# Values of three leading blocks by SyncE's queue, and the first 230 tasks in a new order

## The chip, the core and the metric
The kernel runs on one core of a Trainium2 chip. Its engines are PE (TensorE: matrix products and transposes into PSUM), ACT (ScalarE), DVE (VectorE), POOL (GpSimd) and SP (SyncE, which here only issues DMAs). A DMA issued by POOL is written by software and can cast fp32 to bf16 on its way; one issued by SP or ACT goes through the hardware's queue and leaves the type as it is. All of them use the same 16 DMA engines. The metric is device microseconds of one launch; lower is better.

## The reference
Attention with a sliding window of 128 positions and a linear bias by distance, for 8 batches, 8 heads, 576 positions, head size 64; its output goes through a two-layer network with a squared ReLU.

```python
scores = scale * np.matmul(q, k.transpose(0, 1, 3, 2))
rel = pos[:, None] - pos[None, :]
bias = slopes[:, None, None] * (-np.abs(rel).astype(np.float32))[None, :, :]
mask = (rel >= 0) & (rel < window)
scores = np.where(mask, scores + bias[None], -1000000000.0)
...
attn = np.exp(scores)
attn = attn / (np.sum(attn, axis=-1, keepdims=True) + 1e-09)
attn_out = np.matmul(attn, v).astype(np.float32)
...
x = np.ascontiguousarray(attn_out.transpose(0, 2, 1, 3)).reshape(B * S, H * D)
h = x @ w_in                       # [4608, 512] x [512, 2048]
g = np.maximum(h, 0.0) ** 2
out = (g @ w_out).astype(np.float32)   # [4608, 2048] x [2048, 512]
```

## The kernel before
All of it is one program. The tokens are cut into blocks of up to 128 positions of one batch with all 8 heads. For a block, K, Q and V are loaded as bf16 tiles; K and Q are turned (on PE for the first eight blocks, by DMA for later ones), scores and values follow, and the normalised x [128, 512] is turned for the network. There groups of 512 tokens are multiplied by w_in, pass ReLU and square, and are multiplied by w_out.

Every piece of work is a task, `plan.add({engine: cost}, key, emit, deps, slots to take, slots to give back)`. Nothing is scheduled at run time: the string `ORDER` (lines 62 to 200) names all 1709 tasks in one order, with the engine of each (`a` ACT, `d` DVE, `g` POOL, `s` SP, nothing for PE) and the PSUM banks or buffers that it takes. Each engine's instructions stand in that order, and an engine waits at an instruction until what it needs is there, with everything behind it.

The names of the tasks that matter here, for a block m:
- `lk`, `lq`, `lv`: the loads of K, Q and V. For block 0, `lk0.r` and `lq0.r` go by SP's and ACT's queues in fp32, in halves and in pieces of 1 KB, into a staging tile (a part of `wsum`, which has no other use until much later), and `ck0`, `cq0` cast them. All other loads go by POOL's queue with the cast in the DMA. A tile is 128 positions of 8 heads of 64: 1024 pieces of 256 B in fp32. V lands in `vf`, which also has a column of ones per head.
- `tp m.i` (L690): K (i = 0) or Q (i = 1) turned on PE into a bank; `ev m.i` (L428 on DVE, L430 on ACT): the copy to `kqf`.
- `b m` (L805): the biases of a block into two banks, and `s m` (L814): its scores on top of them. This is the function `lone`, for blocks 0 to 3, which are the first of a batch's positions and look only at themselves.
- `e m.r` (L823): the exponentials to P; `pv m.h` (L874): P times V; `r`, `n` (L888, L901): the reciprocal of the sum and the product that gives x; `xp` (L921): x turned; `x m`: its copy to `xT`.
- `w_in n`: w_in in five pieces, two of 256 columns and three of 512; `u g.r.e` (L1021): for 128 tokens r of group g the up products with piece e of that row; for row 0, `u0.0.0` and `u0.0.1` need w_in 0 and w_in 1, for the other rows `u0.r.0` needs both of these and `u0.r.1` needs w_in 2.

PE's order before begins: warm-up, b0, tp0.0, tp2.0, b2, tp0.1, tp2.1, tp3.0, tp1.0, s2, s0, b1, tp1.1, pv2.0, pv0.0, pv0.1, s1, tp3.1, xp0, pv2.1, pv1.0, pv1.1, b3, u0.0.1, xp2, s3, u0.0.0, xp1, u0.2.0.

POOL's DMAs take turns on eight semaphores, so that POOL waits at a load for the one eight before it. PSUM has eight banks; a task that takes a bank waits for whoever reads it last.

Of the kernel before, what the change touches and what calls it, by code (L numbers as in the profile page):

```python
# [63 lines left out]
slope1.1:d slope0.1:a slope1.3:a ck0:a slope0.2:a warm::0 b0::1,2 lk2:g lq2:g lq0.0:s lq0.1:s lk1:g cq0:a one0.0:d  # L64
tp0.0::0 tp2.0::3 b2::4,5 tp0.1::6 tp2.1::7 ev2.0.0:d ev0.1.0:a lk3:g lq1:g tp3.0::3 ev3.0.0:a ev2.1.0:d ev0.0.0:d
one0.2:d tp1.0::6 s2 s0 e0.0:a e2.0:a e2.1:a ev1.0.0:d e0.1:a lv0:g lv2:g lq3:g lv1:g w_in1:g w_in0:g w_in2:g lv3:g
w_in3:g lk4:g lq4:g b1::0,3 tp1.1::6 pv2.0::4 ev1.1.0:d r2.0:d pv0.0::6 pv0.1::2 s1 n2.0:d r0.1:d r0.0:d n0.0:d
tp3.1::4 n0.1:d xp0.0::2 pv2.1::6 x0.0:d r2.1:d ev3.1.0:d mask1.1:a e1.0:a e1.1:a table:a pv1.0::0 pv1.1::3 b3::5,1
n2.1:d u0.0.1::2 r1.0:d r1.1:d n1.0:d n1.1:d xp2.0::6 s3 u0.0.0::0 xp1.0::3 dist0:d x2.0:a e3.0:a x1.0:a mask1.7:a
reluu0.0.0:a:0 u0.2.0::6 mask0.3:a mask1.2:a mask0.1:a mask1.6:a e3.1:a u0.1.0::3 u0.1.1::0 pv3.0::1 pv3.1::5  # L70
u0.2.1::4 u0.0.2::7 squ0.0.0:d one1.2:d reluu0.1.0:a:0 mask0.2:a reluu0.2.0:a:1 one1.8:d r3.0:d squ0.1.0:d one1.7:d
r3.1:d n3.0:d n3.1:d xp3.0::5 x3.0:d one1.5:d reluu0.2.1:a:0 one1.6:d squ0.2.1:d squ0.2.0:d reluu0.1.1:a:2 mask1.5:a
mask1.4:a mask0.7:a mask0.5:a mask1.3:a mask1.0:a reluu0.0.2:a:3 u0.1.2::0 tp4.0::5 tp4.1::7 ev4.1.0:d squ0.0.2:d
u0.2.2::4 ev4.0.0:a reluu0.0.1:a:1 s4.0::7,2 s4.1::5,1 reluu0.1.2:a:0 e4.0:a lk5:g reluu0.2.2:a:3 lk6:g lq5:g lv5:g
lq6:g w_in4:g tp5.0::0 u0.0.3::6 u0.3.0::4 tp5.1::7 squ0.0.1:d one1.1:d one1.0:d squ0.1.2:d ev5.0.0:d e4.1:a mask0.0:a
mask0.4:a mask0.6:a m4.0:d ev5.1.0:d squ0.1.1:d lk7:g lv4:g lv6:g lq7:g w_out3:g w_out0:g lv7:g w_out2:g w_out1:g
e4.3:a reluu0.3.0:a:0 e4.2:a reluu0.0.3:a:1 squ0.3.0:d u0.3.1::2 tp6.0::7 reluu0.3.1:a:0 ev6.0.0:d tp6.1::4 s5.0::5,1
# [238 lines left out]
def kernel(  # L316
    ctx: ExitStack, tc: tile.TileContext, q, k, v, moe_w_in, moe_w_out, out
):
    nc = tc.nc
# [243 lines left out]
    def load_block(m, key, v_key=None):  # L563
# [56 lines left out]
        def fetch_v():  # L620
            nc.gpsimd.dma_start(tile_of(s_v[m])[0:n, :, 0:D], source(v, m))  # L621
# [859 lines left out]
```

## Time and profile before

| | |
|---|---|
| median of 3 runs | 287.59 us (287.37 to 289.48) |
| the profiled execution | 288.0 us, its span from the first to the last instruction 285.9 us |
| granted TensorE clock | 0.997 |
| PE busy | 277.0 us, 97% of the span |
| DVE busy | 247.1 us, 86% |
| ACT busy | 207.5 us, 73% |
| POOL busy | 106.3 us, 37% |

The difference of 2.1 us between the profiled execution's time and its span lies before the first and behind the last instruction. The shares are means over the whole program; the change lies in the first 25 us, in which PE starts its warm-up at 2.5 us and useful work at 7.5 us. The times of the profile are microseconds from the start of the span. A row of the timeline gives a start, a duration, the engine, the line, the operation and the tiles, and in brackets the idle time before it and who ended it; consecutive instructions of one kind share a row.

### The profile page before, as it was taken

To read this page: it belongs to the slowest core of one execution; us is meant where nothing else is said; L and a number is where in the kernel's file an instruction comes from. 1 tells how busy PE (TensorE), PEld (TensorE's weight loads), DVE (VectorE), ACT (ScalarE), POOL (GpSimd) and SP (SyncE) were. 2 spreads that over 40 slices of the span, in tenths; PEclk is the share of its full clock that TensorE was granted. 3 is DMA by queue.
4 is the path that set the end of the run, shared out by engine and by line. 5 is a ranking of instruction groups with operands and counts; after the bars stand their busy time and mean duration, and the time that the engine had idled before them with its cause. 6 is when DMAs were issued, how large, how long until landed. Compare 5 with 4: busy or idle time off the path is not lost.

```text
span 285.9 us, 8500 instructions
## 1 busy us (share of the span) xinstructions
PE 277.0 (97%) x3403; PEld 240.0 (84%) x3404; DVE 247.1 (86%) x566; ACT 207.5 (73%) x408; POOL 106.3 (37%) x132
## 2 busy tenths in 40 slices
...
GB/s 126 161 197 167 183 201 165 171 172 148 206 145 250 131 172 129 149 207 130 203 135 150 139 174 164 170 164 157 148 93 39 40 73 3 0 111 39 53 79 127
DMA packets 169062, 39.08 MB, mean 137 GB/s; under 512 B 154560, under 2 KB 169024, under 8 KB 169024
## 3 DMA queue, kind: packets, MB, share of 16 engines
...
q8 instruction: 26, 0.43, 0.7%
q10 hardware_dynamic: 592, 0.46, 0.6%
q14 instruction: 12, 0.10, 0.1%
...
## 4 chain that ended last, share of the span: by engine, by line
PE 95%; ACT 2%; DVE 1%; issue 0%; POOL 0%; DVEq 0%; POOLq 0%
PE o L1271 38%; PE h L1116 30%; PE h L1021 9%; PE s L745 6%; PE pv L874 5%; PE wm L662 2%; PE xp L921 1%; PE tp L690 1%; ACT P L823 1%; ACT rt L988 1%; PE pv L856 1%; PE o L1373 0%; PE s L805 0%; ACT masks L475 0%; PE pv L851 0%; PE s L814 0%
## 5 line engine op out<-in xcount | busy, mean ns | idle before, releaser
L1271 PEld LDWEIGHTS <-g 128*128 128x128 bf16 x704 | 67.3, 98 | 9.0
L777 ACT ACTIVATE P<-s 128x512 bf16<-128x512 f32 x120 | 64.7, 613 | 5.7 <-PE s L745 3.3
L430 ACT ACTIVATE f<-h 128x512 f32<-128x512 f32 x74 | 42.5, 601 | 25.8 <-PE h L1116 25.5
L1137 DVE CUSTOM_DVE_ANT_0 rt<-h,f 128x512 bf16<-128x512 f32 x84 | 56.4, 684 | 4.9 <-ACT f L430 1.7
L980 ACT ACTIVATE g<-rt 128x512 bf16<-128x512 bf16 x79 | 48.4, 634 | 6.4 <-DVE rt L1137 5.9
L1271 PE MATMUL o<-w_out_sb,g 128*128 128x256 bf16 x432 | 52.3, 273 | 0.0
L1116 PE MATMUL h<-xT,w_in_sb 128*128 128x256 bf16 x336 | 46.9, 273 | 0.0
L1116 PEld LDWEIGHTS <-w_in_sb 128*128 128x128 bf16 x448 | 42.2, 98 | 5.6
...
L988 ACT ACTIVATE rt<-h 128x512 bf16<-128x512 f32 (+1 forms) x61 | 35.2, 599 | 8.6 <-PE h L1116 3.9
L1271 PE MATMUL o<-wsum,sums 128*128 128x256 bf16 x288 | 35.5, 273 | 0.0
L1116 PEld LDWEIGHTS <-us 128*128 128x128 bf16 x336 | 31.9, 98 | 4.3 <-DVE ut L1085 0.2
L1271 PE MATMUL o<-wsum,g 128*128 128x256 bf16 x272 | 34.5, 273 | 0.0
L772 DVE TENSOR_TENSOR P<-P,masks 128x1024 bf16<-128x1024 bf16 x48 | 32.2, 680 | 1.3 <-ACT masks L475 0.8
L1116 PE MATMUL h<-ut,us 128*128 128x256 bf16 x224 | 31.1, 273 | 0.0
L1021 PE MATMUL h<-xT,w_in_sb 128*128 128x128 bf16 (+1 forms) x384 | 30.8, 237 | 0.1
L982 DVE TENSOR_TENSOR g<-rt 128x512 bf16<-128x512 bf16 (+1 forms) x66 | 26.1, 413 | 4.7 <-ACT rt L988 4.4
L1271 PEld LDWEIGHTS <-sums 128*128 128x128 bf16 x288 | 27.5, 98 | 3.1
L901 DVE TENSOR_TENSOR x<-pv,rec 128x256 bf16<-128x256 f32 x72 | 28.7, 417 | 0.7
L1021 PEld LDWEIGHTS <-w_in_sb 128*128 128x128 bf16 x384 | 27.0, 98 | 2.3 <-issue 0.2
L621 POOL DMA_DIRECT2D vt<-in_v_dram x28 | 25.0, 908 | 7.8 <-PE pv L856 5.3
L430 ACT ACTIVATE f<-o 128x512 f32<-128x512 f32 x29 | 17.3, 599 | 11.0 <-PE o L1271 10.0
...
## 6 DMA issues: line engine op xcount, KB each, us to landing
out_dram<-f SPq DMA_DIRECT2D x62, 128.0 KB, 3.9
kq<-in_k_dram POOLq DMA_DIRECT2D x31, 128.0 KB, 6.4
kq<-in_q_dram POOLq DMA_DIRECT2D x31, 128.0 KB, 7.2
vt<-in_v_dram POOLq DMA_DIRECT2D x28, 128.0 KB, 7.5
w_out_sb<-in_moe_w_out_dram POOLq DMA_DIRECT2D x4, 512.0 KB, 11.6
w_in_sb<-in_moe_w_in_dram POOLq DMA_DIRECT2D x3, 512.0 KB, 8.6
...
vf<-in_v_dram POOLq DMA_DIRECT2D x4, 128.0 KB, 4.9
```

The costliest lines, as they stand in the source:

```text
L430: nc.scalar.activation(o, i, AF.Copy)
L621: nc.gpsimd.dma_start(tile_of(s_v[m])[0:n, :, 0:D], source(v, m))
L772: nc.vector.tensor_tensor(flat(Pt[sP.idx], w), flat(Pt[sP.idx], w), flat(mk, w), op=ALU.mult)
L777: nc.scalar.activation(flat(Pt[sP.idx], slice(2 * i, 2 * i + 2)), sS[i].tile.rearrange("p (j t) -> p j t", j=2)[:, :, lo:hi], AF.Exp, bias ...
L901: nc.vector.tensor_tensor(o, heads(sv)[0:n, :, 0:D], sr.tile[0:n, :].unsqueeze(2).to_broadcast([n, 4, D]), op=ALU.mult)
L980: nc.scalar.activation(o, i, AF.Square, bias=0.0, scale=1.0)
L982: nc.vector.tensor_tensor(o, i, i, op=ALU.mult)
L988: nc.scalar.activation(rts[srt.idx][:, 0:n], slot.tile[:, 0:n], AF.Relu, bias=0.0, scale=1.0)
L1021: nc.tensor.matmul(slot.tile[:, f * w:(f + 1) * w], w_in_sb[:, cc, fc * 128:(fc + 1) * 128], xT[:, cc, lo % (XR * 128):lo % (XR * 128) + w ...
L1116: nc.tensor.matmul(slot.tile[:, j * 256:j * 256 + 256], a, b_, start=fresh and j == 0 and c == 0, stop=c == 1, skip_group_check=True)
L1137: nc.vector._custom_dve(TENSOR_ADD_SAT, out=rts[srt.idx], in0=slot.tile, in1=other(), s0=FMAX, s1=0.0)
L1271: nc.tensor.matmul(slot.tile[:, z * 256:z * 256 + 256], stationary(c), moving(c), start=fresh and z == 0 and c == 0, stop=c == F - 1, skip ...
```

## The change
A constant `V_HW = (0, 2, 1)` names three blocks. For these, `load_block` no longer issues V by POOL; SP issues it in fp32 into one of the three staging tiles that were free, and a new task `cv` casts it to `vf`. Blocks 0, 2 and 1 get stages 1, 2 and 3. K and Q of block 0 stay as they are, but `cq0` is on DVE now and not on ACT.

```diff
+V_HW = (0, 2, 1)
...
         def fetch_v():
             nc.gpsimd.dma_start(tile_of(s_v[m])[0:n, :, 0:D], source(v, m))
+        if m in V_HW:
+            st, s_sv = stages[1 + V_HW.index(m)][:, 0:d_model], Slot(f"stage{1 + V_HW.index(m)}")
+            l_v = plan.add({"SP": 720.0}, key + 0.2 if v_key is None else v_key,
+                           lambda: nc.sync.dma_start(st[0:n].rearrange("s (h d) -> s h d", h=H), source(v, m)), [],
+                           [s_sv], dma=700.0, lat=1500.0, name=f"lv{m}")
+            c_v = plan.add({"DVE": 590.0, "ACT": 480.0}, key + 0.2 if v_key is None else v_key,
+                           lambda: copy(c_v, tile_of(s_v[m])[0:n, :, 0:D], st[0:n].rearrange("s (h d) -> s h d", h=H)),
+                           [l_v], [s_v[m]], [s_sv], name=f"cv{m}")
+            t_load[m] = c_v
+            t_v[m] = [c_v, t_one["v0", m]]
+            return
         l_v = plan.add({"POOL": 890.0}, key + 0.2 if v_key is None else v_key, fetch_v, [], [s_v[m]],
```

The string `ORDER` is written anew for about the first 230 tasks; behind them the order is the same, with other bank and buffer numbers. Two lines of it, from the first loads to the scores of block 2:

```diff
+cq0:d tp0.0::0 tp0.1::3 cv2:d cv0:a tp2.0::4 tp2.1::5 ev2.1.0:d one0.2:d lk3:g ev0.1.0:a ev0.0.0:a lv1:s lq3:g w_in1:g
+w_in0:g w_in2:g lv3:g w_in3:g lk4:g lq4:g ev2.0.0:d b2::6,7 s0 e0.0:a e0.1:a b3::4,0 s2 one0.0:d pv0.0::1 tp1.0::5
```

PE's order now begins: warm-up, b0, tp0.0, tp0.1, tp2.0, tp2.1, b2, s0, b3, s2, pv0.0, tp1.0, tp1.1, tp3.0, b1, pv2.1, pv2.0, pv0.1, s1, xp2, pv1.0, xp0, tp3.1, pv1.1, u0.2.0, u0.0.1, s3, u0.0.0, xp1, u0.2.1. Bias 3 takes banks 4 and 0, of which 4 held tp2.0. Later on, a touch of ACT's table moves from block 1's exponentials to block 7's, and three of the four w_out loads go behind the load of K and Q of block 8.

On DVE, at its first copies, there stood (kqf<-tp is a copy of turned K or Q, the MEMSETs write ones in vf):

```order
9 L513 TENSOR_SCALAR sums<-sums 128x128
10 L522 MEMSET vf 128x8
11 L428 COPY kqf<-tp 128x512 x3
12 L522 MEMSET vf 128x8
13 L428 COPY kqf<-tp 128x512 x2
14 L888 RECIPROCAL rec<-pv 128x4
15 L901 TENSOR_TENSOR x_114<-pv,rec 128x4x64
```

and now:

```order
9 L514 TENSOR_SCALAR sums<-sums 128x128
10 L429 CAST kq_71<-wsum 128x2x4x64
11 L429 CAST vf<-wsum 128x8x64
12 L429 COPY kqf<-tp 128x512
13 L523 MEMSET vf 128x8
14 L429 COPY kqf<-tp 128x512
15 L523 MEMSET vf 128x8
16 L429 COPY kqf<-tp 128x512 x2
17 L900 RECIPROCAL rec<-pv 128x4
18 L913 TENSOR_TENSOR x_114<-pv,rec 128x4x64
```

Rows 10 and 11 are `cq0` and `cv2`; the copies in rows 12 and 14, both of block 2, stand behind them. On ACT, where the copies of block 0 are now, there stood from its first cast on:

```order
4 L430 ACTIVATE kq_71<-wsum 128x2x4x64
5 L515 ACTIVATE sums<-sums 128x128
6 L430 ACTIVATE kq_71<-wsum 128x2x4x64
7 L430 ACTIVATE kqf<-tp 128x512 x2
8 L823 ACTIVATE P_111<-s_154 128x512
9 L823 ACTIVATE P_112<-s_175 128x512
10 L823 ACTIVATE P_112<-s_177 128x512
11 L823 ACTIVATE P_111<-s_156 128x512
```

and now:

```order
4 L431 ACTIVATE kq_71<-wsum 128x2x4x64
5 L516 ACTIVATE sums<-sums 128x128
6 L431 ACTIVATE vf<-wsum 128x8x64
7 L431 ACTIVATE kqf<-tp 128x512 x2
8 L835 ACTIVATE P_111<-s_154 128x512
9 L835 ACTIVATE P_111<-s_156 128x512
10 L835 ACTIVATE P_112<-s_204 128x512
11 L835 ACTIVATE P_112<-s_206 128x512
12 L431 ACTIVATE vf<-wsum 128x8x64
```

Row 6 is `cv0` in the place of `cq0`, and the two copies of row 7 are both of block 0 (before, of blocks 3 and 0). Rows 8 and 9 are block 0's exponentials, now together and ahead of block 2's; row 12 is `cv1`. On POOL the loads ahead of w_in were

```order
8 L610 DMA kq_72<-in_k_dram 128x8x64
9 L610 DMA kq_72<-in_q_dram 128x8x64
10 L610 DMA kq_73<-in_k_dram 128x8x64
11 L610 DMA kq_74<-in_k_dram 128x8x64
12 L610 DMA kq_73<-in_q_dram 128x8x64
13 L621 DMA vf<-in_v_dram 128x8x64 x2
14 L610 DMA kq_74<-in_q_dram 128x8x64
15 L621 DMA vf<-in_v_dram 128x8x64
16 L543 DMA w_in_sb<-in_moe_w_in_dram 128x4x256 x2
```

and are

```order
8 L611 DMA kq_72<-in_k_dram 128x8x64
9 L611 DMA kq_72<-in_q_dram 128x8x64
10 L611 DMA kq_73<-in_k_dram 128x8x64
11 L611 DMA kq_73<-in_q_dram 128x8x64
12 L611 DMA kq_74<-in_k_dram 128x8x64
13 L611 DMA kq_74<-in_q_dram 128x8x64
14 L544 DMA w_in_sb<-in_moe_w_in_dram 128x4x256 x2
```

The three V loads left for SP, where they stand in the order 0, 2, 1 right behind block 0's Q (kq_72, 73 and 74 are blocks 2, 1 and 3).

More of the change, by code (lines that the diff above doesn't have):

```diff
@@ L63 @@
 iota:g ident:d dist1:d slope1.0:d warm0:d lk0.1:a lk0.0:s one0.1:d slope0.3:d slope1.2:a slope0.0:a one0.3:d
[L64 to L77, printed above, removed]
@@ L198 @@
-st8.7.3:s st7.3.0:s st7.3.1:s p8.3.0 p8.3.1 p8.4.0::3 p8.4.1::7 p8.4.1b::0 c12_8:d st8.3.1:s c21.1.0_8:d c21.0.0_8:d
-st8.4.1:s st8.4.0:s st8.3.0:a c21.1.128_8:d st8.4.1b:a
+slope1.1:d slope0.1:a slope1.3:a ck0:a slope0.2:a warm::0 b0::1,2 lk2:g lq2:g lq0.0:s lq0.1:s lv0:s lv2:s lk1:g lq1:g
+cq0:d tp0.0::0 tp0.1::3 cv2:d cv0:a tp2.0::4 tp2.1::5 ev2.1.0:d one0.2:d lk3:g ev0.1.0:a ev0.0.0:a lv1:s lq3:g w_in1:g
+w_in0:g w_in2:g lv3:g w_in3:g lk4:g lq4:g ev2.0.0:d b2::6,7 s0 e0.0:a e0.1:a b3::4,0 s2 one0.0:d pv0.0::1 tp1.0::5
@@ new lines @@
+e2.0:a e2.1:a ev1.0.0:d tp1.1::3 ev1.1.0:d tp3.0::2 cv1:a r0.0:d n0.0:d b1::5,6 pv2.1::7 pv2.0::3 pv0.1::1 s1 r2.1:d
+r2.0:d n2.0:d n2.1:d e1.0:a e1.1:a r0.1:d ev3.0.0:d n0.1:d xp2.0::7 pv1.0::5 xp0.0::1 tp3.1::6 x2.0:d pv1.1::7 r1.0:d
+x0.0:d u0.2.0::2 ev3.1.0:a u0.0.1::6 s3 r1.1:d n1.0:d n1.1:d e3.0:a e3.1:a u0.0.0::7 xp1.0::5 x1.0:d u0.2.1::1 dist0:d
+reluu0.0.0:a:0 reluu0.2.0:a:1 reluu0.2.1:a:2 pv3.1::0 pv3.0::7 u0.0.2::5 u0.1.1::1 reluu0.0.2:a:3 mask0.2:a mask0.4:a
+mask1.2:a r3.1:d squ0.2.0:d squ0.2.1:d r3.0:d one1.5:d one1.6:d mask1.5:a mask1.6:a mask0.1:a mask1.7:a reluu0.1.1:a:2
@@ new lines @@
+mask1.3:a reluu0.0.1:a:1 u0.1.0::5 one1.7:d n3.0:d squ0.0.2:d one1.8:d n3.1:d squ0.0.1:d mask0.5:a u0.2.2::0 mask1.1:a
+reluu0.1.0:a:3 xp3.0::6 reluu0.2.2:a:1 mask1.0:a x3.0:d squ0.1.1:d u0.1.2::1 tp4.0::6 tp4.1::0 reluu0.1.2:a:2
+mask0.6:a ev4.0.0:a ev4.1.0:d squ0.0.0:d squ0.1.0:d squ0.1.2:d u0.3.0::5 reluu0.3.0:a:0 s4.1::6,0 s4.0::1,7 lk5:g
+lq5:g lk6:g lq6:g w_in4:g lv4:g lv5:g lv6:g lk7:g lq7:g lv7:g e4.0:a mask0.0:a mask0.7:a e4.3:a mask0.3:a e4.1:a
+e4.2:a mask1.4:a tp5.0::2 tp5.1::5 u0.3.2::4 u0.0.3::1 reluu0.0.3:a:2 ev5.1.0:d squ0.2.2:d one1.3:d one1.4:d
@@ new lines @@
+squ0.3.0:d ev5.0.0:d s5.0::2,7 tp6.0::6 tp6.1::0 w_out0:g u0.3.1::5 e5.0:a e5.1:a reluu0.3.2:a:0 m4.1:d one1.2:d
+ev6.0.0:d one1.1:d one1.0:d ev6.1.0:d m4.0:d reluu0.3.1:a:1 squ0.3.1:d m5.0:d s5.1::6,2 e5.2:a s6.1::0,1 s6.0::7,3
+e5.3:a e6.0:a e6.2:a e6.1:a e6.3:a u0.2.3::4 pv4.1::5 pv4.0::6 u0.1.3::2 pv5.0::7 m5.1:d r4.0:d n4.0:d tp7.0::0
+pv5.1::6 u0.0.4::3 tp7.1::1 reluu0.2.3:a:1 ev7.0.0:a reluu0.0.4:a:3 ev7.1.0:a r5.0:d r4.1:d squ0.0.3:d r5.1:d m6.0:d
+n5.0:d n5.1:d n4.1:d u0.3.3::4 m6.1:d xp5.0::3 xp4.0::5 pv6.0::1 reluu0.3.3:a:2 x4.0:a squ0.0.4:d x5.0:d squ0.2.3:d
@@ new lines @@
+pv6.1::6 r6.0:d squ0.3.2:d squ0.3.3:d S1.0.0:d s7.0::4,0 reluu0.1.3:a:3 r6.1:d e7.0:a e7.1:a table:a m7.0:d us0.0:d
+s7.1::5,7 e7.3:a e7.2:a n6.0:d m7.1:d us3.0:d n6.1:d squ0.1.3:d us0.1:d S3.0.0:d us2.0:d u1.0.2::3 u1.0.0::4 u1.0.6::0
+u1.0.4::5 reluu1.0.4:a:2 squ1.0.4:a u1.0.1::1 reluu1.0.0:a:3 squ1.0.0:a xp6.0::5 pv7.1::6 r7.1:d pv7.0::7 r7.0:d
+n7.0:d n7.1:d u1.0.7::2 u1.0.5::4 lkq8:g w_out3:g w_out2:g w_out1:g lkq12:g kqT8:s kqT12:s lkq9:g kqT9:s lkq10:g
+xp7.0::6 x7.0:a u1.0.3::7 S2.0.0:d x6.0:d reluu1.0.7:a:3 squ1.0.7:d us1.0:d us1.1:d us3.1:d reluu1.0.1:a:2 u1.1.6::6
@@ new lines @@
+reluu1.0.6:a:0 reluu1.1.6:a:3 squ1.0.6:a squ1.0.1:d us2.1:d reluu1.0.2:a:1 reluu1.0.3:a:0 squ1.0.2:a u1.1.3::2
+u1.1.1::0 u1.1.4::6 reluu1.1.4:a:2 pm1:d pm2:d ws0.0:d squ1.0.3:a u1.1.5::7 u1.1.2::6 squ1.1.6:a reluu1.1.2:a:3
+squ1.1.2:d S1.0.1:d reluu1.1.3:a:0 S2.0.1:d squ1.1.4:a u1.1.0::3 u1.1.7::6 reluu1.1.1:a:3 squ1.1.1:a pm0:a us3.3:d
+us1.3:d reluu1.1.5:a:3 reluu1.1.0:a:2 squ1.1.5:a reluu1.0.5:a:1 squ1.0.5:a p0.2.0::2 p0.2.1 p1.1.0::0 p0.1.0::1 p1.1.1
+p0.1.1 us0.2:d ws1.0:d ws0.1:d ws0.3:d S3.0.1:d p0.5.0::4 ws0.2:d us2.3:d us0.3:d ws1.1:d ws1.3:d us2.2:d S4.0.1:d
@@ new lines @@
+p1.3.0 p1.3.1 m13.1:d ut2.1:d c22_1:d f2.0.5::2 pv13.1::5 pv13.0::3 m15.0:d c12_1:d ut2.2:d r13.0:d r13.1:d m14.0:d
+n13.0:d m14.1:d n13.1:d lkq17:g lv15:g lv16:g lkq18:g st0.7.2:s st0.7.3:s st0.3.1:s kqT17:s st1.7.3:s st1.7.2:s
+st0.3.0:s s15.1::7,1 s16.0::4,6 e16.0:a e16.1:a s5.2.0:a:2 p1.4.0 pv14.0::3 f2.0.1::4 f2.0.2::6 pv14.1::5 s1.2.0:a:7
+r14.0:d n14.0:d m16.0:d e15.3:a e15.2:a c11.2.0:d:0 ut2.3:d r14.1:d m15.1:d f2.0.3 pv15.0::3 f2.0.6 s2.2.0:a:7
+f2.1.1::1 s16.1::6,7 f2.0.7 p1.4.1 c12.2.0:d:2 e16.2:a e16.3:a c22.2.0:d:1 r15.0:d pv15.1::7 f2.1.2::2 f2.1.5::6
@@ new lines @@
+m25.0:d m24.0:d p3.6.0 pv23.0::0 p3.6.1 p3.5.0::7 f4.0.1::4 f4.0.2::6 p3.5.1 f4.1.1::3 pv23.1::2 f4.1.2::5 s1.4.0:a:1
+c11.4.0:d:3 ut4.0:d ut4.1:d r23.0:d r23.1:d lv25:g lkq27:g lkq28:g lv24:g f4.1.5::6 sqc11.4.0:a s1.4.1:a:1 s5_3:a:2
+m25.1:d ut4.2:d c11.4.1:d:3 f4.1.6 f4.0.6 s2.4.1:a:3 s5.4.1:a:4 p3.3.0 s2.4.0:a:1 f4.1.7 f4.0.5::5 f4.0.7 n23.0:d
+S3.3.1:d n23.1:d c22.4.1:d:1 sqc11.4.1:a s5.4.0:a:4 S3.3.0:d ut4.3:d pv25.1::2 p3.3.1 pv25.0::0 f4.0.3 c22.4.0:d:3
+r25.0:d n25.0:d r25.1:d n25.1:d sqc22.4.1:a s2_3:a:4 c12.4.0:d:1 c12_3:d f4.1.3 f4.1.4 reluf4.1.4:a:2 f4.0.4
@@ new lines @@
+sqf4.1.4:d s26.0::2,0 f4.2.1::3 pv24.1::5 reluf4.0.4:a:0 e26.0:a st2.7.2:s st2.3.1:s st2.7.3:s st2.3.0:s st2.4.3:s
+st2.4.2:s kqT27:s x22:s kqT28:s pv24.0::4 s1.4.2:a:1 f4.2.2::7 f4.3.1::2 p3.7.0 sqc12.4.0:a r24.1:d r24.0:d n24.0:d
+c11.4.2:d:2 n24.1:d sqc22.4.0:a e26.1:a sqf4.0.4:a s26.1::5,7 s27.0::0,4 f4.2.6 p3.7.1 c12.4.1:d:3 sqc12.4.1:d
+S1.4.0:d s2.4.2:d:3 m26.0:d S2.4.0:d c22_3:d e26.3:a e27.0:a e26.2:a s1.4.3:a:1 s28.1::0,7 s28.0::5,6 f4.2.7 f4.3.6
+e28.0:a e27.1:a e28.1:a lv26:g lkq30:g lkq32:g lkq31:g lv27:g lv28:g x23:s kqT30:s x25:s x24:s kqT32:s kqT31:s
@@ new lines @@
+sqf5.1.4:a s5.5.3:a:5 reluf5.2.4:a:0 f5.3.7 c12_4:d c12.5.2:d:1 S2.5.0:d S3.5.0:d c22.5.3:d:2 s33.0::0,2 s33.1::4,1
+pv31.0::5 r31.0:d e33.0:a e33.2:a e33.3:a sqf5.2.4:a p4.4.1 f5.3.3 pv32.0::4 sqc22.5.2:d n31.0:d m33.1:d r32.0:d
+sqc22.5.3:a e33.1:a f5.3.4 c12.5.3:d:2 p5.1.0::1 pv32.1::5 pv31.1::2 s3_4:a:5 n32.0:d r31.1:d r32.1:d n31.1:d
+sqc12.5.3:d n32.1:d reluf5.3.4:a:0 sqf5.3.4:a p5.1.1 s34.0::6,4 s35.0::2,3 s34.1::7,0 sqc12.5.2:d m33.0:d S1.5.1:d
+p5.2.0::5 p5.2.1 ut6.0:d lkq36:g lkq38:g lkq37:g lv34:g lv38:g lv36:g lv37:g kqT36:s e34.0:a e34.2:a e35.0:a e35.1:a
@@ new lines @@
+s2.6.3:a:3 f6.3.7 r37.1:d f6.2.6 p5.4.1 f6.2.5::6 e38.2:a s5.6.3:a:1 c22.6.3:d:2 m38.1:d r37.0:d n37.0:d n37.1:d
+s2.6.2:a:2 sqc11.6.2:a f6.2.7 f6.3.3 st4.4.3:s x31:s x32:s st5.2.1:s st5.2.0:s st4.3.0:s x33:s st4.3.1:s st4.4.2:s
+x34:s s5.6.2:a:1 c22.6.2:d:0 f6.2.3 sqc22.6.3:a sqf6.0.4:a c12.6.2:d:2 c12.6.3:d:3 f7.0.1::5 pv38::7,4 s3_5:a:1
+sqc12.6.2:a f6.3.4 f7.1.1::1 pv36.0::2 r38.0:d n38.0:d r38.1:d n38.1:d reluf6.3.4:a:2 sqf6.1.4:d sqf6.3.4:a s1.7.0:a:3
+f7.0.2::7 f6.2.4 reluf6.2.4:a:1 p6.1.0::4 f7.2.1::0 s1.7.2:a:2 s1.7.1:a:5 sqc12.6.3:a sqf6.2.4:a sqc22.6.2:d S2.6.0:d
@@ new lines @@
+ut7.0:d ut7.1:d ut7.2:d r36.0:d m36.1:d c11.7.0:d:0 p6.1.1 f7.2.5::3 f7.2.6 pv36.1::6 f7.0.6 s5.7.2:a:3 f7.1.6
+S1.6.1:d n36.0:d r36.1:d sqc11.7.0:a s2.7.2:a:0 n36.1:d S2.6.1:d s1_6:a:6 st5.3.1:s st5.3.0:s st5.7.3:s x35:s x37:s
+st5.4.3:s x38:s f7.2.3 x36:s p6.2.0::2 p6.2.1 f7.2.7 f7.1.5::6 f7.1.2::7 c12.7.2:d:0 ut7.3:d c11_6:d c11.7.1:d:1
+c22.7.2:d:3 s5.7.1:a:0 f7.3.1::2 f7.1.3 p6.6.0 sqc11.7.1:a s1.7.3:a:5 s2.7.1:a:3 st5.4.2:s st6.2.1:s st6.2.0:s
+st5.7.2:s f7.0.5::7 f7.2.4 f7.1.7 c12.7.1:d:1 s2.7.0:a:7 f7.3.2::3 f7.3.6 p6.5.0::6 c22.7.1:d:2 s5.7.0:d:3 f7.0.3
```

198 lines of the change are left out of this document (78 added, 120 removed).

## The prediction
> **What bounds the kernel now.** I read the chain that ended last and PE's list of waits first. The chain gives 95% of the span to PE; the list says when PE stood still.
>
> ```profile
> PE 95%; ACT 2%; DVE 1%; issue 0%; POOL 0%; DVEq 0%; POOLq 0%
> ```
>
> ```profile
> PE wm L662 <- DVE sums L448: 2.5, 1, 2.5
> PE pv L874 <- ACT P L823: 1.0, 2, 0.6
> PE xp L921 <- DVE x L901: 0.5, 1, 0.5
> PE tp L690 <- ACT rt L988: 0.4, 1, 0.4
> ```
>
> The first wait is the time before the warm-up, which the change leaves alone. The others are the only real ones, and pv, which reads V, waits for P from ACT, not for V. PE's timeline shows where they lie (start, duration, then the idle time before).
>
> ```profile
> 7.50 0.60 PE L805 MATMUL s<-sums,ident 128*128 128x512 bf16 x2
> 7.93 0.61 PE L690 MATMUL tp<-ident,kq 128*128 128x128 bf16 x8
> ...
> 9.88 0.38 PE L690 MATMUL tp<-ident,kq 128*128 128x128 bf16 x4 [0.24 <-ACT kqf L430]
> ...
> 12.11 0.42 PE L874 MATMUL pv<-vf,P 128*128 128x65 bf16 x8 [0.41 <-ACT P L823]
> 13.09 0.29 PE L874 MATMUL pv<-vf,P 128*128 128x65 bf16 x4 [0.56 <-ACT P L823]
> ...
> 14.52 0.40 PE L921 MATMUL xp<-ident,x 128*128 128x128 bf16 x4 [0.48 <-DVE x L901]
> ...
> 17.51 2.84 PE L1021 MATMUL h<-xT,w_in_sb 128*128 128x128 bf16 x48
> 20.19 0.41 PE L874 MATMUL pv<-vf,P 128*128 128x65 bf16 x8
> 20.43 1.95 PE L1021 MATMUL h<-xT,w_in_sb 128*128 128x128 bf16 x32
> ...
> 24.33 0.38 PE L690 MATMUL tp<-ident,kq 128*128 128x128 bf16 x4 [0.39 <-ACT rt L988]
> ```
>
> Starts give prices without the modelled ends: two bias products 7.93 - 7.50 = 0.43 us; a 128-column product (17.51 to 20.19, 48 of them) 0.056; a value product (20.19 to 20.43, 8) 0.03. Between 7.50 and 17.51 PE does 8 bias products (1.72), 32 transposes of K and Q (1.79), 32 scores (1.79), 24 values (0.72), 12 transposes of x (0.67) and 16 up products (0.90): 7.6 of 10.0 us, so it idles 2.4 us. Later there is the 0.39 and one of about 0.2. Some 3 us is the ceiling of any gain here, 1% of the time; and since PE has no further stall, each microsecond gained or lost before 18 us reaches the end whole.
>
> The second limit is the loads. Issue start plus time to landing:
>
> ```profile
> 1.48 1.23 SPq L585 DMA_DIRECT2D wsum<-in_q_dram  x2
> ```
>
> ```profile
> 2.35 0.89 POOL L610 DMA_DIRECT2D kq<-in_q_dram  x1
> ...
> 8.41 0.95 POOL L621 DMA_DIRECT2D vf<-in_v_dram  x1
> 9.28 2.31 POOL L543 DMA_DIRECT2D w_in_sb<-in_moe_w_in_dram  x3
> ```
>
> ```profile
> wsum<-in_q_dram SPq DMA_DIRECT2D x1, 128.0 KB, 4.2
> kq<-in_q_dram POOLq DMA_DIRECT2D x1, 128.0 KB, 5.0
> vf<-in_v_dram POOLq DMA_DIRECT2D x1, 128.0 KB, 4.8
> w_in_sb<-in_moe_w_in_dram POOLq DMA_DIRECT2D x2, 256.0 KB, 6.0
> w_in_sb<-in_moe_w_in_dram POOLq DMA_DIRECT2D x1, 512.0 KB, 8.2
> ```
>
> Block 0's second Q half lands at 2.1 + 4.2 = 6.3. q2 lands at 2.35 + 5.0 = 7.35, v1 at 8.41 + 4.8 = 13.2; between them lie seven tiles, 0.84 us each, though POOL issues one in 0.9: the engines run without a gap. w_in0, issued at about 10.1, lands near 16.4 (the 6.0 is the median of two), w_in2, issued at about 10.9, near 19.1.
>
> **The change, part by part.** *The bytes.* Three V tiles leave POOL's queue for SP's. Ahead of w_in still stand nine tiles, so with full engines w_in0 and w_in2 land where they did, 16.4 and 19.1; only the order among the nine changes. What share SP's queue gets sets that order. Beside each other and alone the queues did this (first fence 4.5 to 5.5 us, second 2.5 to 3.5, third 4.5 to 6.3; q1 is SP's, q10 ACT's, q0 POOL's):
>
> ```profile
> q0 software_dynamic: 694, 0.09, 137.0%
> q1 hardware_dynamic: 133, 0.12, 44.0%
> ```
>
> ```profile
> q1 hardware_dynamic: 182, 0.17, 53.7%
> q10 hardware_dynamic: 144, 0.13, 38.5%
> ```
>
> ```profile
> q0 software_dynamic: 1631, 0.21, 179.1%
> q1 hardware_dynamic: 148, 0.13, 26.7%
> ```
>
> Alone, the hardware queues moved 326 one-KB pieces in a microsecond; beside POOL's, 133, which is 41% of that pace. POOL's kept 694 of its 1024 / 0.84 = 1219, 57%. V's pieces are 256 B, not 1 KB, and no row shows those from SP here, so the price of a V tile is an estimate. By this share it is 0.84 / 0.41 = 2.0 us. The near end is half, 1.7. The far ends: by bytes of the longer window (148 KB in 1.8 us, 256 KB a tile) 3.1 us; by pieces, 133 to 694, a sixth of 1219, 5.2 us. I take 2.0, because in the 1 us window both queues have work throughout, while at the end of the longer one SP's runs dry. Behind 6.3 that puts v0 at 8.3, v2 at 10.3, v1 at 12.3 (before: v0 10.7, v2 11.6, v1 13.2).
>
> The Trainium skill, DMA: Bandwidth & Descriptors, section Queues, rings and completion order, has each DMA engine go round the queues that have work, one packet at a time, which for equal packets is the half. By it v2 lands 0.6 us earlier and the sum below ends at about 288.2. The trace's 41% is near it, with other pieces.
>
> *What waits for V now.* Before, nobody but pv. Now a cast does, and it stands in line ahead of copies that PE needs. Prices:
>
> ```profile
> 6.41 0.63 ACT L430 ACTIVATE kq<-wsum 128x512 bf16<-128x512 f32 x1 [1.50 <-DMA wsum<-in_q_dram]
> 9.23 1.09 ACT L430 ACTIVATE kqf<-tp 128x512 bf16<-128x512 bf16 x2 [2.20 <-PE tp L690]
> 10.97 2.06 ACT L823 ACTIVATE P<-s 128x512 bf16<-128x512 f32 x4 [0.65 <-PE s L814]
> ```
>
> ```profile
> 9.46 1.36 DVE L428 COPY kqf<-tp 128x512 bf16<-128x512 bf16 x3 [0.46 <-PE tp L690]
> ...
> 13.42 0.25 DVE L888 RECIPROCAL rec<-pv 128x4 f32<-128x4 f32 x2 [0.34 <-PE pv L874]
> 13.71 0.76 DVE L901 TENSOR_TENSOR x<-pv,rec 128x256 bf16<-128x256 f32 x2
> ```
>
> A cast on ACT is 0.63. DVE's fp32 cast does not occur before; it lies between its bf16 copy, 1.36 / 3 = 0.45, and ACT's 0.63: I take 0.55. Moving block 0's Q cast from ACT to DVE thus costs nothing on PE's path: DVE is idle there.
>
> Step by step. Bias 0, the sixteen transposes of blocks 0 and 2 and bias 2 keep PE until 7.50 + 0.43 + 0.90 + 0.43, about 9.3.
> 1. ACT: cv0 waits for v0, 8.35 to 9.0; the two copies of block 0 behind it 1.09, to 10.1. Scores 0 start at 10.15. PE waits **0.85**.
> 2. DVE: cv2 waits for v2, 10.35 to 10.9; the copies of block 2 behind it 2 x 0.45, to 11.8. Bias 3 takes the bank that one of them empties, so it starts at 11.85, and on PE scores 2 and pv0.0 are queued behind it. Scores 0 ended at 10.6: PE waits **1.25**.
> 3. Bias 3, scores 2, pv0.0, three transposes (0.67) and bias 1 run to 14.0; block 2's exponentials, 2 x 0.51 in a row and a tail, end at 13.95, and pv2.1 follows without much loss. DVE has the copies of block 1, one reciprocal and product for block 0 (to 14.55) and two of each for block 2 (0.25 + 0.76) ahead of xp2: it starts at 15.6. After scores 1 PE was free at 14.75. It waits **0.85**.
> 4. xp0 needs one more reciprocal, copy and product on DVE, about 1.05: 16.65, against 15.95 free. **0.7**.
> 5. u0.2.0 starts near 17.2, behind w_in0's 16.4; u0.0.1, scores 3, u0.0.0 and xp1 follow, and u0.2.1 at about 19.65 is behind w_in2's 19.1: **0**.
>
> That is 3.65 us of waits instead of 2.4: **+1.2 us**. Block 0's chain is earlier, scores 0 stand near 10.15 instead of about 10.5, but block 2's, now behind it, gives that back and more. If V came faster, the sum could fall only to u0.2.1's w_in2: the work up to it takes PE to 17.51 + 0.9 = 18.4 with the old waits, so a landing at 19.1 leaves +0.7. Both limits have the same sign.
>
> *Costed at nothing.* cv1 on ACT (0.63), behind block 2's exponentials, lies in time in which ACT has no scores. The ACT table's touch and the reordered w_out loads are moved where PE has tens of microseconds of other work. POOL issues w_in 2.7 us earlier, into engines that have no gap; if they had one, w_in would land up to 2.5 us (three tiles) earlier. SP has nothing behind the V loads that is wanted before w_in has landed. Bank numbers behind the first tasks are only permuted.
>
> The profiled run is 288.0 with a span of 285.9; the median is 287.6. So 289.2 by the profile, **288.8** by the median.
>
> **Rivals.**
> *SP's queue gets little.* If V costs 3.1 us a tile, v2 lands at 12.5, 2.2 us later, and step 2's wait grows by all of it, since bias 3 is queued ahead of everything: +3.4, 291.0. It turns a 1% loss when a V tile costs about 2.9 us. At 5.2, v2 is at 16.7: +7.6, 295. For it: the 148 pieces in 1.8 us; against: SP ran out there, and the 41%.
> *The order pays.* If V's pieces are cheaper than POOL's and fit in at 7.0, 8.0, 9.0, step 1 falls to 0.35, step 2 to 0, steps 3 and 4 to about 0.8 each: 1.95, a gain of 0.45, but only if w_in0 lands by 15.3 and not 16.4: 287.1. For it: POOL issues w_in earlier; against: 0.84 us a tile with no gap.
> *V is hidden.* PE never waited for V, so moving it may show nothing: 287.3 to 288.0. Against it: the casts stand ahead of PE's copies.
>
> **How the numbers follow.** Forecast, +0.6 to +1.9 (half share to 2.4 us a tile): 0.47. Little for SP: 0.30. Order pays: 0.13, and 0.03 of it by over 1%. Hidden: 0.10. A measurement tells about 1%, 2.9 us, from no change. Slower by more: nearly all of the second case and the tail of the first, 0.30; faster 0.03; same 0.67. The range leaves out the worst of SP's shares and the best of the order: 287.0 to 291.8.
>
> **What would show it.** SP's V loads landing near 8.3, 10.3, 12.3; DVE's cast of vf beginning where the second lands, with idle time before it named for that load; PE's list with about 1.2 us at bias 3 for DVE, and 0.7 to 0.9 at xp twice; w_in2 still near 19. The prediction is wrong if v2 lands before 9 or after 12, if PE's first wait is for K or Q from POOL, or if PE gains stalls behind 25 us.

## The result, and the profile after

The changed kernel takes 291.04 us (median of seven runs, 290.22 to 295.16), beside 287.75 us for the kernel before: a ratio of 1.0105, with an interval of 1.0071 to 1.0138. It is slower by some 3.0 to 3.3 us, where 1.2 were forecast; the time lies inside the range, near the price of the first rival. Medians here are over all runs, ratios over undisturbed ones, each against runs of the kernel before made beside it (medians 287.6 to 288.1 us). The profiled execution took 291.36 us with a span of 289.3, 3.4 us longer than before.

The chain of the page, and PE's list of waits, of the changed kernel:

```profile
PE 90%; DMA 3%; ACT 2%; POOL 1%; DVE 1%; issue 1%; DVEq 0%; POOLq 0%
```

```profile
PE s L817 <- DVE vf L523: 1.8, 1, 1.8
PE s L826 <- ACT kqf L431: 1.0, 1, 1.0
PE xp L933 <- ACT rt L1000: 0.3, 1, 0.3
PE tp L702 <- DMA kq<-in_k_dram: 0.3, 1, 0.3
PE xp L933 <- DVE x L913: 0.3, 1, 0.3
```

The wait for P is gone, and the two largest are those of steps 2 and 1: bias 3 for DVE, scores 0 for ACT. The row of bias 3 names a MEMSET (L523), of which DVE has one behind each copy of block 2; the second copy, which empties the bank that bias 3 takes, ends at 12.8, where bias 3 starts. A DMA, which had no share of the chain before, has 3%. It is the load of K of block 3, from its issue to its landing at 14.74 (start, duration):

```profile
4.97 9.77 DMA kq<-in_k_dram
```

The timeline, of PE, of ACT's cast of v0, and of DVE's casts of block 0's Q and of v2:

```profile
10.64 0.40 PE L826 MATMUL s<-kqf 64*128 64x128 bf16 x8 [0.98 <-ACT kqf L431]
12.85 0.61 PE L817 MATMUL s<-sums,ident 128*128 128x512 bf16 x2 [1.81 <-DVE vf L523]
...
14.79 0.61 PE L702 MATMUL tp<-ident,kq 128*128 128x128 bf16 x4 [0.33 <-DMA kq<-in_k_dram]
15.19 1.06 PE L817 MATMUL s<-sums,ident 128*128 128x512 bf16 x2
...
17.75 0.54 PE L933 MATMUL xp<-ident,x 128*128 128x128 bf16 x4 [0.31 <-DVE x L913]
...
21.51 1.06 PE L1033 MATMUL h<-xT,w_in_sb 128*128 128x128 bf16 x16
```

```profile
8.98 0.63 ACT L431 ACTIVATE vf<-wsum 128x512 bf16<-128x512 f32 x1 [4.00 <-DMA wsum<-in_v_dram]
```

```profile
6.65 0.43 DVE L429 CAST kq<-wsum 128x512 bf16<-128x512 f32 x1 [3.92 <-DMA wsum<-in_q_dram]
11.39 0.73 DVE L429 CAST vf<-wsum 128x512 bf16<-128x512 f32 x1 [4.31 <-DMA wsum<-in_v_dram]
```

Both casts of V start on the landing of their V: v0 at about 9.0, v2 at 11.4. v1, issued last, at 4.4, and 10.4 us under way, lands at 14.8. u0.2.1, the last row of PE's, starts at 21.5. The work ahead of it was done at 18.4 in the kernel before (17.5 and the 0.9 of u0.2.0): 3.1 us of the 3.4 are lost by there.

The third reading is the loads that stayed with POOL: three rows of its timeline, and the time to landing of K of block 2, Q of block 3, the first two pieces of w_in and w_in2, which u0.2.1 reads.

```profile
1.36 1.02 POOL L611 DMA_DIRECT2D kq<-in_k_dram  x1 [0.18 <-issue]
...
5.83 0.93 POOL L611 DMA_DIRECT2D kq<-in_q_dram  x1
6.70 2.29 POOL L544 DMA_DIRECT2D w_in_sb<-in_moe_w_in_dram  x3
```

```profile
kq<-in_k_dram POOLq DMA_DIRECT2D x1, 128.0 KB, 5.0
kq<-in_q_dram POOLq DMA_DIRECT2D x1, 128.0 KB, 9.6
w_in_sb<-in_moe_w_in_dram POOLq DMA_DIRECT2D x2, 256.0 KB, 10.3
w_in_sb<-in_moe_w_in_dram POOLq DMA_DIRECT2D x1, 512.0 KB, 12.5
```

The first POOL tile lands at 6.4, as before, and the last of the nine leading tiles at 5.83 + 9.6 = 15.4: 9.0 us for eight tiles that took 6.8. w_in was issued 2.6 us earlier and lands later: w_in2 at 8.17 + 12.5 = 20.7 instead of about 19.0. Five of the eight are POOL's, at 0.84 us; that leaves (9.0 - 4.2) / 3 = 1.6 us for a V tile on SP's queue, against 0.84 on POOL's. By w_in's first piece, which lands at 6.70 + 10.1 = 16.8 instead of 15.0, it is 0.84 + 1.8 / 3 = 1.4. In the new order u0.2.1 cannot start before w_in2 is in: 20.7 - 18.4 = 2.3 of the 3.1 us stand by this landing alone.

### The profile page after: what moved, and what is told of

Read it like the earlier page. It is cut to its first block, busy times and chain, and to the rows that moved or that the text cites. A ratio compares the mean times of both kernels' runs of the same rounds, so it can differ in the third digit from the quotient of the medians.

```text
span 289.3 us, 8513 instructions
## 1 busy us (share of the span) xinstructions
PE 278.6 (96%) x3404; PEld 240.8 (83%) x3404; DVE 248.0 (86%) x569; ACT 207.9 (72%) x408; POOL 103.7 (36%) x129
## 4 chain that ended last, share of the span: by engine, by line
PE 90%; DMA 3%; ACT 2%; POOL 1%; DVE 1%; issue 1%; DVEq 0%; POOLq 0%
PE o L1283 38%; PE h L1128 30%; PE h L1033 8%; PE s L757 6%; PE pv L886 5%; DMA kq<-in_k_dram 3%; POOL kq L611 1%; PE xp L933 1%; ACT masks L476 1%; PE tp L702 1%; ACT P L789 1%; PE pv L868 1%; PE o L1385 0%; DVE x L913 0%; PE pv L863 0%
## 5 line engine op out<-in xcount | busy, mean ns | idle before, releaser
L617 POOL DMA_DIRECT2D kq<-in_k_dram x24 | 21.5, 894 | 59.2 <-DMA kqT<-kq 55.6
L994 DVE TENSOR_TENSOR g<-rt 128x512 bf16<-128x512 bf16 x66 | 26.4, 415 | 5.9 <-ACT rt L1000 5.5
## 6 DMA issues: line engine op xcount, KB each, us to landing
w_in_sb<-in_moe_w_in_dram POOLq DMA_DIRECT2D x3, 512.0 KB, 12.5
```

What stands on the lines that cost most here:

```text
L994: nc.vector.tensor_tensor(o, i, i, op=ALU.mult)
```

## The experiments

Two theories were set against each other: the **casts** (DVE and ACT stand at a cast with PE's copies behind it) and the **loads** (a V tile on SP's queue costs the DMA engines about 1.5 us and delays all loads). The **order** itself and the **clock** came beside them.

### The order alone (e1)
V back on POOL's queue, the new order otherwise.

```diff
-V_HW = (0, 2, 1)
+V_HW = ()
-... lq0.1:s lv0:s lv2:s lk1:g lq1:g cq0:d tp0.0::0 tp0.1::3 cv2:d cv0:a ... lv1:s ... cv1:a
+... lq0.1:s lv0:g lv2:g lk1:g lq1:g cq0:d tp0.0::0 tp0.1::3 ... lv1:g ...
```

> The new order with V of blocks 0, 2, 1 back on POOL's queue (behind lq2, and lv1 behind lk3), so no casts of V. Loads theory (a V tile through SP's queue costs the DMA engines about 1.5 us, not 0.84, and delays everything behind it): w_in0 and w_in2 land at 16.4 and 18.9 again, bias 3 does not wait over 0.3 us, 288.0 to 288.4 us. Casts theory (what costs is that DVE and ACT stand at a cast): the same, since the casts are gone. Order theory (the new order itself is the loss): 290 us or more.

288.98 us, ratio 1.0034 (1.0011 to 1.0057). The list of waits of this run:

```profile
PE h L1033 <- DMA w_in_sb<-in_moe_w_in_dram: 1.8, 2, 1.1
PE xp L933 <- DVE x L913: 0.8, 2, 0.6
PE tp L702 <- DMA kq<-in_k_dram: 0.4, 1, 0.4
```

Bias 3 does not wait, but PE is ahead of w_in now and waits for that: the new order asks for w_in2 with u0.2.1 sooner than the old one did.

```profile
19.82 1.07 PE L1033 MATMUL h<-xT,w_in_sb 128*128 128x128 bf16 x16 [1.08 <-DMA w_in_sb<-in_moe_w_in_dram]
```

The wait ends at w_in2's landing, 10.8 + 9.0 = 19.8, which is 0.9 us later than the 18.9 expected; why, no run shows. Even with V on POOL's queue the new order thus holds u0.2.1 back by 19.8 - 18.4 = 1.4 us. So the order alone loses a third of a per cent, 0.6 us more than was expected of it, and is not the bulk.

### The queue alone (e5)
The order of before, V on SP's queue, the casts behind most of what PE needs.

```diff
-lq0.1:s ... ev1.0.0:d e0.1:a lv0:g lv2:g lq3:g lv1:g ... e1.1:a
+lq0.1:s lv0:s lv2:s lv1:s ... ev1.0.0:d cv2:d e0.1:a cv0:a lq3:g ... e1.1:a cv1:a
```

> The order of before with the three V loads on SP's queue, and their casts at places where little stands behind them: block 2's on DVE behind block 1's K copy, block 0's and block 1's on ACT behind the exponentials. Loads theory: w_in0 and w_in2 land 1.5 to 2 us later than before, 289.2 to 290.2 us. Casts and order theories: 287.5 to 288.2 us.

292.22 us, ratio 1.0141 (1.0105 to 1.0177), 2 us above even the loads theory's figure. Its waits:

```profile
PE tp L702 <- DMA kq<-in_k_dram: 3.7, 1, 3.7
PE wm L674 <- DVE sums L449: 2.5, 1, 2.5
PE pv L886 <- ACT vf L431: 1.4, 2, 1.0
```

The old order has block 3's first transpose ahead of scores 2 and 0, so its K, late now, stops PE for 3.7 us. Behind that wait the granted clock is 0.50 from 13 to 15 us, which is in the time too; how much of the 2 us it is, was not separated. The new order makes good part of what the queue costs: 1.05% with it, 1.41% without.

### The casts out of the way (e2)

```diff
-cq0:d tp0.0::0 tp0.1::3 cv2:d cv0:a ... ev0.0.0:a ... ev1.0.0:d
+cq0:d tp0.0::0 tp0.1::3 ... ev0.0.0:a cv0:a ... ev1.0.0:d cv2:d
```

> The change with the cast of block 0's V behind ACT's copies of block 0 and the cast of block 2's V behind DVE's copies of block 2 and block 1's K. Casts theory: bias 3's wait of 1.8 us and the wait at scores 0 go, the clock stays at 1.00, 288.5 to 289.0 us. Loads theory: PE stops instead at tp3.0, whose K lands near 14.7, and u0.2.1 can't start before w_in2 at about 20.7, so 290.0 to 290.8 us, within 0.6 us of the change's runs beside it.

291.2 us, ratio 1.0095 (1.0062 to 1.0129): the time of the changed kernel. Its waits:

```profile
PE tp L702 <- DMA kq<-in_q_dram: 2.2, 2, 1.2
PE tp L702 <- DMA kq<-in_k_dram: 1.7, 1, 1.7
PE xp L933 <- DVE x L913: 0.8, 2, 0.6
PE xp L933 <- ACT rt L1000: 0.3, 1, 0.3
PE h L1033 <- DMA w_in_sb<-in_moe_w_in_dram: 0.3, 1, 0.3
```

The waits for casts are gone, and 3.9 us of waits for K and Q by POOL have come in their place. At u0.2.1 PE waits until w_in2 lands, 8.16 + 13.5 = 21.7:

```profile
21.73 1.07 PE L1033 MATMUL h<-xT,w_in_sb 128*128 128x128 bf16 x16 [0.28 <-DMA w_in_sb<-in_moe_w_in_dram]
```

So the casts do not make the loss: they were what PE stood at, with the late loads right behind them. In this profiled execution the clock stays at 1.00 and the time is 291.02 us, so it is not made by the half clock either.

### The loads without their casts (e4)
The kernel before, plus three V loads on SP's queue that nobody reads.

```diff
+        if m in (0, 1, 2):
+            st = stages[1 + m][:, 0:d_model]
+            plan.add({"SP": 720.0}, key, lambda: nc.sync.dma_start(st[0:n].rearrange("s (h d) -> s h d", h=H), source(v, m)),
+                     [], [], dma=700.0, name=f"xv{m}")
```

> The kernel before, and behind block 0's Q on SP's queue three more loads of V in fp32 into the idle staging tiles, which nobody reads. Loads theory: w_in2 lands 4 to 5 us later than 18.9 (three times about 1.5 us), K, Q and V of the leading blocks 2 to 4 us later, 290.5 to 292 us. Prediction's price of 0.84 us a tile: w_in2 2.5 us later, 289 to 290 us. Casts theory: no cast stands in a line, so within 0.4 us of before.

292.23 us, ratio 1.0142 (1.0105 to 1.0179). v1 by POOL and the first piece of w_in, issued at 8.4 and 9.28 as before:

```profile
vf<-in_v_dram POOLq DMA_DIRECT2D x1, 128.0 KB, 9.3
w_in_sb<-in_moe_w_in_dram POOLq DMA_DIRECT2D x1, 256.0 KB, 9.8
```

Before, the V tile took 4.8 and that piece 5.7. The loads are 4.5 and 4.1 us later, 1.4 to 1.5 us for each of the three. With not one instruction more on PE, DVE or ACT, the kernel loses 4.3 us (here twelve tiles stand ahead of w_in, not nine). The loads are the only thing added, but not all of the 4.3 us is waiting: behind a wait of 3.1 us for K of block 3 the clock, the column behind the five engines, falls.

```profile
13.00:19.00 6.00, 4.44 (x49) 2.90 (x45) 2.07 (x8) 3.43 (x8) 4.05 (x5) 0.50 1.87 173
```

### The same bytes in pieces of 1 KB (e8)

```diff
+        if m in (1, 2, 3):
+            for r in range(2):
+                plan.add({"SP": 720.0}, key, lambda r=r: nc.sync.dma_start(view(stages[m], 0, True)[:, r], source(k, m, True)[:, :, r]),
+                         [], [], dma=350.0, name=f"xk{m}.{r}")
```

> The kernel before, and behind block 0's Q on SP's queue six loads of half a K block in fp32, in pieces of 1 KB, into the idle staging tiles, which nobody reads: the same 768 KB as three V tiles, in a quarter of the pieces. Piece theory (the price is per small piece): 0.87 us or less for 256 KB, so w_in1 lands 2 to 2.7 us later than 15.0, 289.3 to 290.5 us. Bytes theory: as with 256 B pieces, w_in1 4 to 4.5 us later, near 292 us.

290.69 us, ratio 1.0065 (1.0040 to 1.0091). The same two loads:

```profile
vf<-in_v_dram POOLq DMA_DIRECT2D x1, 128.0 KB, 7.7
w_in_sb<-in_moe_w_in_dram POOLq DMA_DIRECT2D x1, 256.0 KB, 8.2
```

2.9 and 2.5 us later, 0.8 to 1.0 us for 256 KB. The hardware queues alone moved 326 such pieces in a microsecond, 0.8 us for 256 of them, so these loads cost little more than that beside POOL's. This is near the piece theory's 0.87, though one of the two prices and the median, by 0.2 us, lie above its range.

### The same bytes by POOL (e6)
V in fp32 into the staging tiles and cast there, but issued by POOL at the places of e1, with the casts as in e2 (block 1's behind ACT's exponentials of block 2).

```diff
-            l_v = plan.add({"SP": 720.0}, key + 0.2 if v_key is None else v_key,
-                           lambda: nc.sync.dma_start(st[0:n]...
+            l_v = plan.add({"POOL": 890.0}, key + 0.2 if v_key is None else v_key,
+                           lambda: nc.gpsimd.dma_start(st[0:n]...
```

> The new order with V of blocks 0, 2, 1 loaded by POOL's queue, but in fp32 into the staging tiles and cast there: the bytes and pieces of the change, without its queue. Queue theory (a piece of 256 B through the hardware's queue is dearer than through POOL's): 0.84 us a tile as before, w_in0 near 16.2 and w_in2 near 19.3, 288.5 to 289.5 us. Bytes theory (fp32 writes twice the bytes of bf16, whatever the queue): 1.5 us a tile, w_in0 near 18, w_in2 near 20.7, 290 to 291.5 us.

289.55 us, ratio 1.0042 (1.0012 to 1.0073). w_in's first piece, issued at 9.32, with the time to landing of before:

```profile
9.32 2.33 POOL L544 DMA_DIRECT2D w_in_sb<-in_moe_w_in_dram  x3
```

```profile
w_in_sb<-in_moe_w_in_dram POOLq DMA_DIRECT2D x1, 256.0 KB, 5.7
```

So the bytes of fp32 are not dear by themselves: through POOL's queue the tiles cost what bf16 cost. But the run did not keep the pieces, as was meant. What the 16 engines moved from 5.5 to 13 us:

```profile
DMA packets 5592, 1.57 MB, mean 209 GB/s; under 512 B 5137, under 2 KB 5400, under 8 KB 5592
```

192 packets are of 2 KB or more, and there is none of these in the same stretch of e1. Three V tiles are 768 KB, so these are the V tiles in packets of 4 KB; on SP's queue each piece of 256 B was a packet. Whether POOL's queue would move fp32 in packets of 256 B at 0.84 us a tile, no run shows; its tiles with the cast, in 1024 packets each, take that.

### The clock (e3)
After the two long waits PE's granted clock falls. Windows of the changed kernel:

```profile
9.60:12.80 3.20, 0.46 (x9) 0.23 (x8) 1.41 (x5) 2.07 (x5) 1.25 (x3) 1.00 1.90 162
...
14.00:15.00 1.00, 0.67 (x12) 0.50 (x10) 0.73 (x3) 1.00 (x3) 0.00 (x0) 0.84 1.65 187
15.00:18.00 3.00, 2.69 (x29) 1.78 (x28) 1.97 (x9) 1.00 (x3) 2.46 (x3) 0.50 1.38 201
```

The column behind the five engines is the clock, 0.50 from 15 to 18 us; two bias products took 1.06 us there (row at 15.19), 0.60 before. The experiment fills the wait at bias 3 with products:

```diff
         def biases():
+            if m == 3:
+                bank(sS[1], "s1")
+                for _ in range(8):
+                    nc.tensor.matmul(sS[1].tile, warm[:, 0:128], warm, start=True, stop=True)
```

> The change with eight more warm-up products (128x512, of zeros, into bias 3's second bank) ahead of bias 3, so that PE works in the 1.8 us in which it waits for DVE. Clock theory (the half clock from 14.7 to 18.0 us is a large part of the loss): the clock stays at 1.00 and the time falls by 1.0 to 1.5 us against the change's own runs. Loads theory: the clock may stay at 1.00, but K of block 3 still lands near 14.7 and w_in2 near 20.7, so the time falls by 0 to 0.5 us.

290.8 us, ratio 1.0087 (1.0063 to 1.0110), and in its windows the clock is full:

```profile
10.00:13.00 3.00, 2.23 (x16) 0.93 (x16) 1.41 (x5) 1.80 (x4) 1.08 (x2) 1.00 2.08 157
13.00:18.00 5.00, 4.31 (x65) 2.94 (x66) 3.43 (x14) 2.72 (x5) 2.98 (x4) 1.00 1.42 191
```

The intervals of the two kernels overlap. A gain of 0.2 us lies between the medians, 0.5 between the ratios, and 0.8 between the spans of the two profiled executions (288.5 and 289.3). From bias 3 on PE is faster, by 1.0 us up to u0.2.1:

```profile
13.01 0.60 PE L821 MATMUL s<-sums,ident 128*128 128x512 bf16 x2
...
20.71 1.07 PE L1037 MATMUL h<-xT,w_in_sb 128*128 128x128 bf16 x16
```

But there w_in2 has only just landed, at 8.15 + 12.5 = 20.65. So most of the slow clock was covered by the loads, which allow no earlier start, and at most 0.8 us of the changed kernel's loss is the clock's own.

### A better place for the up products (e7)

```diff
-pv1.1::7 r1.0:d x0.0:d u0.2.0::2 ev3.1.0:a u0.0.1::6 s3 ... u0.0.0::7 xp1.0::5 x1.0:d u0.2.1::1 ... u0.1.0::5
+pv1.1::7 r1.0:d x0.0:d ev3.1.0:a u0.0.1::6 s3 u0.2.0::2 ... xp1.0::5 u0.0.0::7 x1.0:d u0.1.0::3 u0.2.1::1 ...
```

> The new order with V on POOL's queue (no casts), and on PE the first up products in another order: u0.0.1 and scores 3 ahead of u0.2.0, xp1 ahead of u0.0.0, and u0.1.0 ahead of u0.2.1, so that 1.8 us of waits for w_in0 and w_in2 are filled. Loads theory: those waits go, all but 0.2 us, 287.1 to 287.7 us, 0.1 to 0.3% under before. Order theory: 288.3 us or more.

289.25 us, ratio 1.0042 (1.0021 to 1.0062): no better than e1, so the loads theory missed here. The waits for w_in went, as meant, and this came in their place:

```profile
PE h L1033 <- DVE x L913: 1.3, 2, 0.7
```

PE now waits for DVE twice at up products. Why the new order loses 0.3% even without V on SP stays open beyond these rows; no version here beats the kernel before.

### The queue by itself (e9)
Three V tiles by SP, then K halves in 1 KB pieces by SP, then three V tiles by POOL, at about 230 to 249 us, where the DMA engines stand idle in the kernel before.

```diff
-st5.7.2:s
+st5.7.2:s xv0:s xv1:s xv2:s xk2.0:s xk2.1:s xk1.0:s xk1.1:s xk0.0:s xk0.1:s xg0:g xg1:g xg2:g
```

> The kernel before, with twelve loads that nobody reads put into the stretch from about 230 to 250 us in which the DMA engines stand idle: first three V tiles in fp32 by SP (256 KB each, pieces of 256 B), then six halves of K tiles in fp32 by SP (128 KB each, pieces of 1 KB), then three V tiles by POOL with the cast, each group behind the one before. Piece theory (a small piece is dear in the hardware's queue by itself): V tiles by SP follow each other at about 1.5 us, the K halves at 0.4 us. Side-by-side theory (it is dear only while POOL's queue works beside it): V tiles by SP at 1.0 us or less. POOL's tiles at about 0.9 us in both. The time is that of before within 0.5%.

One execution, 287.6 us. The stretch of 232.6 to 235.6 us, in which SP's V tiles are alone:

```profile
GB/s 297 280 297 283 283 287 294 287 283 283 307 283 283 277 222 232 202 198 202 208 219 205 198 212 229 232 212 191 208 215 218 212 191 154 127 85 55 31 0 0
...
q1 hardware_dynamic: 2532, 0.64, 111.6%
```

0.64 MB in 3 us with an end that runs dry; a V tile of 256 KB takes 0.9 us at the 283 GB/s of the first third and 1.3 at the 200 of the next, about 1.0 between landings (234.0, 235.2 and 236.0 us). The same by pieces: 1034 from 233 to 234 us, 836 from 234 to 235, so 1.0 and 1.2 us a tile. So part of the price, above POOL's 0.84, is there when SP's queue is alone, and the side-by-side theory holds only in part: the 1.4 to 1.6 us are reached beside POOL's queue. Why the rate falls from 283 to 200 GB/s, this one execution does not show. The K halves say nothing of their price here, since SP issued one only every 0.8 us (4.84 us for six); POOL's three tiles were issued every 0.88 us.

## Why the prediction was right, and where it was not

**What bounds it: held.** Behind 27 us PE's list shows no wait: a run of 40 up products starts at 42.05 instead of 38.67, and this lag of 3.4 us reached the end whole.

**Steps 1 and 2: the places held, the sizes were low.** Scores 0 waited for ACT behind the cast of v0 (0.98 instead of 0.85), bias 3 for DVE behind the cast of v2 (1.81 instead of 1.25). v0 came at 9.0 instead of 8.3, v2 at 11.4 instead of 10.3. DVE's cast took 0.73 us, above both bounds that I gave it, 0.45 and 0.63; block 0's Q cast, with as many elements, took 0.43, and why the two differ no run shows.

**Steps 3 and 4: mis-sized, by a wait and a clock that were not foreseen.** xp2 waited 0.31 instead of 0.85, and xp0, forecast at 0.7, not at all, since PE itself was late: tp3.0 stood for block 3's K, and then the half clock stretched PE's work. u0.2.1 came at 21.5 instead of 19.65: bias 3 started 1.0 us later than forecast, and the way from there took 8.7 instead of 7.8 us. At full clock, in e3, it took 7.7.

**The step that failed is the first, the bytes.** "With full engines w_in0 and w_in2 land where they did" took a V tile on SP's queue to cost the engines what it costs on POOL's. It cost 1.6 us by the changed kernel's landings and 1.4 to 1.5 by e4's, not 0.84. So the nine tiles were in at 15.4 and not 13.2, and w_in2 at 20.7 and not 19.1. The same row that gave the 41% could not tell: SP's pieces in it were of 1 KB, and e8 shows that these cost 0.8 to 1.0 us for 256 KB. The prediction named that difference and then took the price from the row all the same. By the ratios the new order alone loses 1.0 us (e1) and SP's queue the other 2.0, of which the half clock has 0.2 to 0.8 (e3). The lost 2 us are thus in the main this term. The prediction's second limit, w_in2's landing, gave +0.7 at 19.1 and gives +2.3 at 20.7, above the +1.2 of the casts, and e2 shows that without any cast in the way PE stops at the same late loads for the same total. So the waits that made up the forecast's +1.2 came where they were put, but taking them away saves nothing. That the time lies inside the range is in part luck: the range reaches that far because of a small share for SP's queue, not because POOL's loads come late. The measured 1.05% is just past the 1% beyond which the prediction gave 0.30.

**The rivals.** "SP's queue gets little" had the right time, 291.0, from a V tile of 3.1 us; measured are 2.4 us between v0 and v2 and 3.4 between v2 and v1, 2.8 in the mean behind 6.3. It had the loss in step 2's wait alone and did not say that POOL's tiles would be late too. "The order pays" fell: w_in0 landed later, not earlier, and the order alone loses 0.34%. "V is hidden" fell with the first row of PE's waits.

**The clock.** PE was busy for 0.5 of 3.2 us from 9.6 to 12.8, and ran at half clock from about 14.7 to 18. The Trainium skill, TensorE: Matmul & The Clock Gate, in its part on the HAM clock gate, states that an idle window of about 3.4 us halves the clock. The trace agrees only in part: the clock fell behind the two long waits, and not in e3, but the longest single wait was 1.81 us; and in e2 PE was busy for as little, and the clock did not fall.

```profile
12.10:15.35 3.25, 0.41 (x6) 0.23 (x5) 1.70 (x5) 0.79 (x3) 1.38 (x2) 1.00 1.58 172
```

So what decides it is more than the share of work in such a stretch, and no run here shows what. It is no main term here, with at most 0.8 us of the loss.
